# Pair 9's x scaled one step earlier, and pair 10's B and C loaded ahead of two stores, in a state-space scan followed by a bilinear feed-forward layer

## The chip, the cores and the metric

One core of one Trainium2 chip runs the whole program. The metric is the device time of one execution, in microseconds (us). Of the kernel before there are four such times: 125.66, 125.97, 127.06 and 128.04 us, with a median of 126.51 us.

## The reference, cut to what matters

The first half is a chunked state-space scan over x (4 batches, 8 heads, 768 tokens, 32 columns), decays a, and B and C (16 states a head). The second half multiplies two projections of its result and projects the product back.

```python
for c in range(nc):                       # chunks of 32 tokens
    cum = np.cumsum(la, axis=-1)          # la: log of the decays
    L = np.exp(cum[:, :, :, None] - cum[:, :, None, :]) * causal
    M = np.einsum('bhin,bhjn->bhij', Cc, Bc) * L
    y_intra = np.einsum('bhij,bhjd->bhid', M, xc)
    y_inter = np.einsum('bhin,bhnd->bhid', Cc, state) * np.exp(cum)[..., None]
    y[:, :, sl] = y_intra + y_inter
    state = decay_full * state + (Bc outer xc, decayed, summed over j)
...
a = x @ w_a          # 3072 tokens x 256 -> 1536
b = x @ w_b
return a * b @ w_out # -> 3072 x 256
```

## The kernel before, in words

**Tiling.** The kernel works with blocks of 128 tokens, so a sequence is six blocks. Two batches with all their heads make one *pair*; there are 12 pairs, 0 to 11, and pairs 2k and 2k+1 belong to block k. From pair 4 on, the path of one pair is this:

- `loads_bc(p)` (L699) allocates the pair's input tiles and issues four DMAs on SP's queue: C for two batches, then B for two batches, 64 KB each. `loads_x(p, nc.sync)` (L142) issues two DMAs of x, 128 KB each. The tiles `bn`, `cn` and `xn` have three buffers each.
- `prep(p)` (L853) works on POOL: C times its factors into `planes` (L279), B times its factors into `bm` (L287), two copies of `bm` into `planes` (L297). Then `turn(p)` (L331) issues one DMA transpose of `planes` on SP's queue, whose result is `turned`.
- `prep_x(p)` (L862) is one POOL instruction (L272): x times a constant, to f16. Its result is the weight operand of the pair's matmuls at L402.
- `stage(p, ...)` (L874) issues the pair's score matmuls on PE (L341), which read `turned`; `masked` multiplies them by the causal mask on DVE (L396) and puts feed-forward units of an earlier block between them (`bu`, `bunit`: matmuls at L650, copy on ACT at L598, product on DVE at L662).
- `group(blk)` (L866) issues, for both pairs of a block, the matmuls with the state (L491), those with x (L402, first all of the even pair and then all of the odd one), and the state's new sums (L430); ACT and DVE move the results to SBUF.
- `bout(blk, c)` (L668) is one output tile: twelve matmuls (L677), a copy on ACT into one of four `osb` buffers (L689), and a store of 128 KB on SP's queue (L690).

**What sets the order.** The schedule is written out by hand: each engine and each queue runs its instructions in the order of the program's text, and an instruction waits by semaphore for the data that it needs. SP's queue carries the loads, the transposes and the stores, one behind another. So a `turn` that waits for POOL holds back every load and store behind it, and a POOL instruction that waits for a load holds back all POOL work behind it.

**Around the change.** The text before runs `prep(9)`, the loads of x of pair 9, the rest of pair 7, `group(3)`, two output tiles `bout(2, 0)` and `bout(2, 1)`, and only then `loads_bc(10)`. After the scores of pair 8 it runs `prep_x(8)`, `prep(10)`, `loads_bc(11)` and `loads_x(10)`. `prep_x(9)` stands in the loop, behind the scores of pair 9 (L977, first round). `group(4)`, which needs x of pairs 8 and 9, follows later in that round.

Of the kernel before, what the change touches and what calls it, by code (L numbers as in the profile page):

```python
# [28 lines left out]
def kernel(  # L29
# [100 lines left out]
    def tiles(p):  # L130
        Bn = inp.tile([128, H, 2, N], f32, name="bn", tag="bn")
        Cn = inp.tile([128, H, 2, N], f32, name="cn", tag="cn")
        Xn = inp.tile([128, H, 2, D], f32, name="xn", tag="xn")
        pair_in[p] = (Bn, Cn, Xn)
# [4 lines left out]
    def load1(eng, p, which, bt, i0=0, n=64):  # L139
        blk, bp = divmod(p, NBP)  # L140
        if p >= P0:
            return eng.dma_start(  # L142
                by_token(pair_in[p][which])[:, bt],
                (B, C, x)[which][2 * bp + bt, :, blk * Q : (blk + 1) * Q, :].rearrange("h q n -> q h n"),
            )
        src = (B, C, x)[which][2 * bp + bt, :, blk * Q + 2 * i0 : blk * Q + 2 * i0 + 2 * n, :]
        return eng.dma_start(
            pair_in[p][which][64 * bt + i0 : 64 * bt + i0 + n].rearrange("i h r n -> i h (r n)"),
            src.rearrange("h (i r) n -> i h (r n)", r=2),
        )  # L150
# [114 lines left out]
    def scale_x(p, eng):  # L265
        X16 = mid.tile([128, H, 2, D], f16, name="x16", tag="x16")
        xo, xi = X16.rearrange("p h r d -> p (h r d)"), pair_in[p][2].rearrange("p h r d -> p (h r d)")
        st.setdefault(p, {})["X16"] = X16
        if eng is nc.scalar:
            nc.scalar.mul(xo, xi, XS)  # L270
        else:
            eng.tensor_scalar(xo, xi, XS, None, ALU.mult)  # L272

    def scale_bc(p, which, eng, factor=None):
        blk, bp = divmod(p, NBP)
        name, f = (("bm", fB), ("cm", fC))[which]
        raw = by_token(pair_in[p][which]) if p >= P0 else pair_in[p][which].rearrange("p h r n -> p r h n")
        if p >= P0 and which:
            eng.tensor_tensor(  # L279
                out=planes[p % 2][:, 4:6].rearrange("p t (h n) -> p t h n", n=N),  # L280
                in0=raw,
                in1=f[:, blk, :, bp].unsqueeze(3).broadcast_to((128, 2, H, N)),
                op=ALU.mult,
            )
            return
        m_ = mid.tile([128, 2, H, N], f16, name=name, tag=name)
        eng.tensor_tensor(  # L287
            out=m_,
            in0=raw,
            in1=(f[:, blk, :, bp] if factor is None else factor).unsqueeze(3).broadcast_to((128, 2, H, N)),  # L290
            op=ALU.mult,
        )
        st.setdefault(p, {})[name] = m_
        if p >= P0:
            dst = planes[p % 2][:, 0:4].rearrange("p (t e) (m f n) -> p t e m f n", e=2, f=2, n=N)
            for e in range(2):
                eng.tensor_copy(dst[:, :, e, :, e], m_.rearrange("p t (m f) n -> p t m f n", f=2)[:, :, :, e])  # L297
# [31 lines left out]
    def turn(p):  # L329
        T_ = mid.tile([128, 6, 128], f16, name="turned", tag="turned")  # L330
        nc.sync.dma_start(T_, planes[p % 2].rearrange("p a c -> p (a c)"), transpose=True)  # L331
        st[p]["BT"] = T_[:, 0:4].rearrange("p (t e) k -> p e t k", e=2)
        st[p]["CT"] = T_[:, 4:6]
# [32 lines left out]
    def product(p, m):  # L366

        if p >= P0:
            return (
                st[p]["T1"][:, 2 * m : 2 * m + 2].rearrange("p e t q -> p (e t) q"),  # L370
                SC[m].rearrange("p (c q) -> p c q", q=Q),
            )
        return (
            st[p]["T1"][:, 2 * m : 2 * m + 2].rearrange("p e r q -> p e (r q)"),
            SC[m].rearrange("p (e c) -> p e c", e=2),
        )
# [8 lines left out]
    def mask(out_in, by_pool=False, by_token=False):  # L385
        o_, i_ = out_in
        if by_token:
            c_ = causal_q.unsqueeze(1).broadcast_to((128, 4, Q))
        else:
            c_ = causal.rearrange("p r q -> p (r q)").unsqueeze(1).broadcast_to((128, 2, 2 * Q))  # L390
        if by_pool:
            tmp = mid.tile([128, *c_.shape[1:]], f32, name="tmp", tag="tmp")
            nc.scalar.copy(tmp, i_)  # L393
            nc.gpsimd.tensor_tensor(out=o_, in0=tmp, in1=c_, op=ALU.mult)  # L394
        else:
            nc.vector.tensor_tensor(out=o_, in0=i_, in1=c_, op=ALU.mult)  # L396
# [155 lines left out]
    def state_spread(p):  # L552
        blk, bp = divmod(p, NBP)
        if p + NBP < P0:
            Sbd = mid.tile([128, 2, H * D], f16, name="sbd", tag="sbd")
            nc.gpsimd.tensor_tensor(
                out=Sbd.rearrange("p t (m c) -> p t m c", m=4),
                in0=U32[:, p].unsqueeze(2).broadcast_to((128, 2, 4, 2 * D)),
                in1=maskbd.rearrange("p (m e) d -> p m (e d)", e=2).unsqueeze(1).broadcast_to((128, 2, 4, 2 * D)),
                op=ALU.mult,  # L560
            )
        else:
            Sbd = mid.tile([128, 2, 2 * D], f16, name="spair", tag="spair")
            nc.gpsimd.tensor_tensor(
                out=Sbd.rearrange("p t (e d) -> p t e d", e=2),
                in0=U32[:, p].rearrange("p t (e d) -> p t e d", e=2),
                in1=par.unsqueeze(1).unsqueeze(3).broadcast_to((128, 2, 2, D)),
                op=ALU.mult,
            )
        if blk + 1 < NG:  # L570
            nc.gpsimd.tensor_tensor(
                out=gU[:, p + NBP],
                in0=U32[:, p],
                in1=G[:, 2 * bp : 2 * bp + 2, blk + 1].unsqueeze(2).broadcast_to((128, 2, 2 * D)),
                op=ALU.mult,
            )
        st.setdefault(("S", p + NBP), {})["Sbd"] = Sbd
# [86 lines left out]
    def bgo(blk, *ks):  # L664
        for k in ks:
            bunit(blk, k)()
# [25 lines left out]
    def loads_bc(p):  # L692
        if p < NP:
            tiles(p)
            for w in (1, 0):
                for bt in range(2):
                    load1(nc.sync, p, w, bt)

    def loads_x(p, eng=None):  # L699
        if p < NP:  # L700
            for bt in range(2):
                load1(eng or nc.gpsimd, p, 2, bt)
# [150 lines left out]
    def prep(p, spread=()):  # L853
        if p < NP:
            scale_bc(p, 1, nc.gpsimd)
            scale_bc(p, 0, nc.gpsimd)
            turn(p)
        for q in spread:
            if q // NBP < NBLK - 1:
                state_spread(q)  # L860

    def prep_x(p):  # L862
        if p < NP:
            scale_x(p, nc.gpsimd)

    def group(blk):  # L866
        for p in range(blk * NBP, (blk + 1) * NBP):
            pull(p)
        outputs(blk)
        if blk < NBLK - 1:  # L870
            for p in range(blk * NBP, (blk + 1) * NBP):
                state_sums(p, (0,))
# [11 lines left out]
    def masked(p, ms, *units):  # L884
        for i in range(max(len(ms), len(units))):
            h = units[i]() if i < len(units) else None
            if i < len(ms):
                mask(product(p, ms[i]), by_token=True)
            if h:
                h()  # L890
# [4 lines left out]
    def bu(blk, *ks):  # L895
        return [lambda k=k: bunit(blk, k) for k in ks]
# [61 lines left out]
    prep(8)  # L958
    prep(9)
    loads_x(9, nc.sync)  # L960
    masked(7, (0, 1, 2), *bu(2, 5, 6, 7, 8, 9, 10, 11))
    group(3)
    bout(2, 0)
    bout(2, 1)
    loads_bc(10)

    stage(8, True, (6, 7))
    prep_x(8)
    prep(10)
    loads_bc(11)  # L970
    loads_x(10, nc.sync)
# [2 lines left out]
    for blk in range(4, NBLK):  # L974
        pB = blk * NBP + 1
        stage(pB, False)
        prep_x(pB)  # L977
        loads_x(pB + 2, nc.sync)
        prep(pB + 2)
        masked(pB, (0, 1))  # L980
        bout(blk - 2, 2)
        masked(pB, (2, 3), *bu(blk - 1, 6, 7, 8, 9))
        group(blk)
        bout(blk - 2, 3)
        bgo(blk - 1, 10, 11)
        if blk + 1 < NBLK:
            stage(pB + 1, False, (pB - 1, pB))
            prep_x(pB + 1)
            masked(pB + 1, (0, 1))
            bout(blk - 1, 0)  # L990
            masked(pB + 1, (2,))
            bout(blk - 1, 1)
            masked(pB + 1, (3,), *bu(blk, 0, 1, 2, 3, 4, 5))
# [40 lines left out]
```

## Time and profile before

| | |
|---|---|
| four runs | 125.66, 125.97, 127.06, 128.04 us, median 126.51 |
| the profiled execution's own time | 125.66 us |
| its span in the profile | 123.9 us |
| PE busy (matmuls) | 118.8 us, 96% of the span |
| PE weight loads | 81.3 us, 66% |
| DVE, ACT, POOL busy | 85.3, 71.9, 67.2 us |
| POOL's x scaling (L272) | 7 instructions, mean 1491 ns |
| granted PE clock | full in all 40 slices |
| x, B and C loads on SP's queue | median 3.6, 3.1 and 3.7 us from issue to landing |
| the transposes on SP's queue | 8, median 3.1 us from issue to landing |

The profile is one execution, and it is the fastest of the four times. Its span leaves out 1.76 us of the execution's time (125.66 less 123.9). Times inside the trace are counted from the span's start. Durations of instructions are those of the hardware; a POOL duration is rough, and the ends of matmuls are modelled, so that gaps on PE are read from the starts. A row of the timeline gives start, duration, engine, line and what is written and read; behind it, in brackets, the idle time before it and what ended it.

### The profile page before, as it was taken

Reading aid. Unit: us, or ns where it says so; the run is one execution under the profiler, and the core shown is the slowest. Engines: PE = TensorE matmul, PEld = TensorE weight load, DVE = VectorE, ACT = ScalarE, POOL = GpSimd, SP = SyncE. Lnnn points to the kernel's source line nnn. Section 1 sums busy time; section 2 is a strip of 40 time slices with the busy share of each in tenths; the row PEclk is TensorE's granted clock in tenths of the full one; section 3 lists DMA queues with packets and bytes.
Section 4 is the critical chain, followed back from the end, with each engine's and each line's share of the span. In section 5 each row is a group of like instructions: output and inputs, shape, how many; then the busy total and the mean of one; then the engine's idle time right before and its main releaser. Section 6 shows DMA issues by size and latency. Waiting matters only on the chain.

```text
span 123.9 us, 3757 instructions
## 1 busy us (share of the span) xinstructions
PE 118.8 (96%) x1455; PEld 81.3 (66%) x1455; DVE 85.3 (69%) x162; ACT 71.9 (58%) x142; POOL 67.2 (54%) x113
## 2 busy tenths in 40 slices
PE   5999999999999999999999999999999999999990
PEld 2446889988889788744457455657464785555880
DVE  1786885785987579398984989847889444847100
ACT  0366754684646685778658756674637736556220
POOL 7999999949999369279942855426800000000000
PEclk9999999999999999999999999999999999999999
DMA  3999999996989699599973862579811012010122
GB/s 67 164 173 232 174 206 160 199 175 61 113 120 195 73 91 211 112 163 132 182 102 68 173 62 27 91 69 146 215 40 42 5 42 85 0 48 0 42 92 78
DMA packets 63153, 13.73 MB, mean 111 GB/s; under 512 B 57904, under 2 KB 62672, under 8 KB 63136
## 3 DMA queue, kind: packets, MB, share of 16 engines
q1 hardware_dynamic: 58800, 9.01, 45.5%
q0 software_dynamic: 2336, 4.13, 18.3%
q10 hardware_dynamic: 2000, 0.36, 1.6%
q8 instruction: 11, 0.18, 0.7%
q14 instruction: 6, 0.05, 0.1%
HBM read 11.13 MB, written 3.15 MB: 115 GB/s over the span
## 4 chain that ended last, share of the span: by engine, by line
PE 76%; POOL 8%; DMA 6%; issue 2%; SPq 2%; ACT 1%; DVE 1%; POOLq 0%; ACTq 0%
PE ops L677 17%; PE aps L650 17%; PE bps L650 17%; PE aps L584 5%; PE bps L584 4%; DMA turned<-planes 4%; PE SC L210 3%; DMA cn<-in_C_dram 2%; PE ops L620 2%; PE SC L341 2%; POOL bm L287 2%; PE fps L238 2%; PE SC L402 1%; SPq L142 1%; POOL x L272 1%
## 5 line engine op out<-in xcount | busy, mean ns | idle before, releaser
L598 ACT COPY asb<-aps 128x512 f32<-128x512 f32 x72 | 42.0, 587 | 14.2 <-PE aps L650 9.7
L662 DVE TENSOR_TENSOR hkb<-bps,asb 128x512 f16<-128x512 f32 x48 | 32.3, 688 | 12.9 <-ACT asb L598 11.8
L650 PE MATMUL aps<-XB,Wa 128*128 128x512 f16 x96 | 28.6, 379 | 0.0
L650 PE MATMUL bps<-XB,Wb 128*128 128x512 f16 x96 | 28.5, 379 | 0.0
L677 PE MATMUL ops<-Wo,hkb 128*128 128x256 f16 (+1 forms) x204 | 22.5, 267 | 0.0
L677 PEld LDWEIGHTS <-hkb 128*128 128x128 f16 x204 | 18.5, 98 | 3.1
L396 DVE TENSOR_TENSOR t<-SC,causal_q 128x512 f16<-128x512 f32 x26 | 16.7, 682 | 5.1 <-PE SC L341 5.1
L605 DVE TENSOR_TENSOR hk<-bps,asb 128x512 f16<-128x512 f32 x24 | 16.2, 684 | 4.1 <-ACT asb L598 3.6
L650 PEld LDWEIGHTS <-Wb 128*128 128x128 f16 x96 | 9.9, 103 | 11.0 <-issue 0.3
L650 PEld LDWEIGHTS <-Wa 128*128 128x128 f16 x96 | 9.7, 103 | 9.1 <-issue 0.2
L584 PE MATMUL aps<-X2T,Wa 128*128 128x256 f16 x96 | 14.3, 273 | 0.3 <-DVE X2T L476 0.3
L689 ACT ACTIVATE osb<-ops 128x256 f32<-128x256 f32 (+1 forms) x16 | 6.0, 377 | 14.4 <-PE ops L677 14.2
L584 PE MATMUL bps<-X2T,Wb 128*128 128x256 f16 x96 | 14.1, 273 | 0.0
L620 PE MATMUL ops<-Wo,hk 128*128 128x256 f16 x96 | 11.6, 273 | 0.0
L272 POOL TENSOR_SCALAR x<-xn 128x512 f16<-128x512 f32 x7 | 10.4, 1491 | 1.4 <-DMA xn<-in_x_dram 1.0
L394 POOL TENSOR_TENSOR t<-tmp,causal_q 128x512 f16<-128x512 f32 x6 | 6.9, 1161 | 7.8 <-ACT tmp L393 7.7
L584 PEld LDWEIGHTS <-Wa 128*128 128x128 f16 x96 | 9.4, 104 | 1.5 <-DVE X2T L476 0.4
L584 PEld LDWEIGHTS <-Wb 128*128 128x128 f16 x96 | 9.8, 103 | 0.7
L620 PEld LDWEIGHTS <-hk 128*128 128x128 f16 x96 | 8.9, 98 | 1.5 <-DVE hk L605 0.2
L279 POOL TENSOR_TENSOR planes<-cn,fC 128x256 f16<-128x256 f32 x8 | 5.0, 624 | 7.2 <-DMA cn<-in_C_dram 7.1
L396 DVE TENSOR_TENSOR t<-SC,causal 128x512 f16<-128x512 f32 x13 | 8.2, 683 | 0.9 <-PE SC L356 0.8
L287 POOL TENSOR_TENSOR bm<-bn,fB 128x256 f16<-128x256 f32 x11 | 7.1, 648 | 2.9 <-DMA bn<-in_B_dram 1.5
(94 smaller groups left out, 124.5 us busy)
## 6 DMA issues: line engine op xcount, KB each, us to landing
out_dram<-osb SPq DMA_DIRECT2D x23, 128.0 KB, 1.9
xn<-in_x_dram SPq DMA_DIRECT2D x13, 128.0 KB, 3.6
bn<-in_B_dram SPq DMA_DIRECT2D x20, 64.0 KB, 3.1
xn<-in_x_dram POOLq DMA_DIRECT2D x10, 128.0 KB, 4.7
cn<-in_C_dram SPq DMA_DIRECT2D x18, 64.0 KB, 3.7
Wa<-in_moe_w_a_dram POOLq DMA_DIRECT2D x2, 384.0 KB, 5.6
Wb<-in_moe_w_b_dram POOLq DMA_DIRECT2D x2, 384.0 KB, 7.0
Wo<-in_moe_w_out_dram POOLq DMA_DIRECT2D x2, 384.0 KB, 6.9
```

What stands on the lines that cost most here:

```text
L272: eng.tensor_scalar(xo, xi, XS, None, ALU.mult)
L287: eng.tensor_tensor(out=m_, in0=raw, in1=(f[:, blk, :, bp] if factor is None else factor).unsqueeze(3).broadcast_to((128, 2, H, N)), op=AL ...
L394: nc.gpsimd.tensor_tensor(out=o_, in0=tmp, in1=c_, op=ALU.mult)
L396: nc.vector.tensor_tensor(out=o_, in0=i_, in1=c_, op=ALU.mult)
L584: nc.tensor.matmul(ps[:, kk * 2 * Q : (kk + 1) * 2 * Q], W[k // 6][:, f, k % 6 // 3 * 384 : (k % 6 // 3 + 1) * 384].rearrange("p (c kk) -> ...
L598: (nc.vector.tensor_copy if on_dve else nc.scalar.copy)(asb, a_ps)
L605: nc.vector.tensor_tensor(out=s["hk"][:, 2 * k2 : 2 * k2 + 2, :].rearrange("p k q -> p (k q)"), in0=b_ps, in1=asb, op=ALU.mult)
L620: nc.tensor.matmul(o_ps[:, 0:d_model], hk[:, k, bt * Q : (bt + 1) * Q], Wo[:, k, :], start=(k == 0), stop=(k == NK - 1), skip_group_check= ...
L650: nc.tensor.matmul(t_, W[k // 6][:, f, k % 6 // 3 * 384 : (k % 6 // 3 + 1) * 384].rearrange("p (c kk) -> p kk c", kk=3)[:, k % 3], XB[:, b ...
L662: return lambda: nc.vector.tensor_tensor(out=s["hk"][:, k], in0=ps[1], in1=asb, op=ALU.mult)
L677: nc.tensor.matmul(o_ps[:, 0:w], hk[:, k, c * Q : (c + 1) * Q], Wo[:, k, cs], start=(k == 0), stop=(k == NK - 1), skip_group_check=True,)
L689: nc.scalar.activation(out=o_sb[:, 0:w], in_=o_ps[:, 0:w], func=AF.Copy, scale=1.0 / (YS * YS))
```

## The change

Three places move; nothing is added and nothing is taken away. `loads_bc(10)` goes ahead of `masked(7, ...)`, `group(3)` and the two output tiles in the text: on SP's queue, its four loads now stand ahead of the two stores of `bout(2, 0)` and `bout(2, 1)`. `prep_x(9)` goes directly behind `prep_x(8)`: on POOL, ahead of pair 10's four instructions instead of behind them. The loop leaves out its own `prep_x` in its first round, since that was pair 9's.

```diff
     prep(8)
     prep(9)
     loads_x(9, nc.sync)
+    loads_bc(10)
     masked(7, (0, 1, 2), *bu(2, 5, 6, 7, 8, 9, 10, 11))
     group(3)
     bout(2, 0)
     bout(2, 1)
-    loads_bc(10)
 
     stage(8, True, (6, 7))
     prep_x(8)
+    prep_x(9)
     prep(10)
     loads_bc(11)
     loads_x(10, nc.sync)
@@
     for blk in range(4, NBLK):
         pB = blk * NBP + 1
         stage(pB, False)
-        prep_x(pB)
+        if blk > 4:
+            prep_x(pB)
         loads_x(pB + 2, nc.sync)
         prep(pB + 2)
```

In the compiled programs the order of instructions differs in two places only: on POOL, the scaling of pair 9's x stands ahead of `planes`, `bm` and two copies of pair 10; on SP, four loads stand ahead of two stores. PE, DVE and ACT run the same instructions in the same order.

## The prediction

> **What bounds the kernel now.** I read the page first: shares of the engines, granted clock and the chain that ended last.
>
> ```profile
> span 123.9 us, 3757 instructions
> ...
> PE 118.8 (96%) x1455; PEld 81.3 (66%) x1455; DVE 85.3 (69%) x162; ACT 71.9 (58%) x142; POOL 67.2 (54%) x113
> ...
> PEclk9999999999999999999999999999999999999999
> ...
> PE 76%; POOL 8%; DMA 6%; issue 2%; SPq 2%; ACT 1%; DVE 1%; POOLq 0%; ACTq 0%
> ```
>
> PE is nearly always busy, at full clock, and three quarters of the chain are its own. Then I read the chain in order of time. From 52.28 us on, up to the last copy on ACT, every piece of it is PE's. So a change in that stretch is worth what it takes out of the gaps between matmuls. Rows of the chain give start, length, engine and line:
>
> ```profile
> 64.12 0.56 PE SC L402 x32
> ...
> 78.66 0.63 PE SC L402 x32
> ...
> 82.55 0.33 PE SC L341 x16
> ...
> 90.79 0.33 PE SC L341 x16
> ...
> 96.24 0.56 PE SC L402 x32
> ```
>
> The 32 matmuls with x take 0.56 us in groups 3 and 5, but 0.63 in group 4. The instructions' starts show why: the 16 of pair 8 begin at 78.59, and the first of pair 9 at 78.89, 0.11 us after the one before it, where this step takes 0.05 in the other groups. PE waited there for x of pair 9. The POOL timeline tells where that came from:
>
> ```profile
> 71.34 1.49 POOL L272 TENSOR_SCALAR x<-xn 128x512 f16<-128x512 f32 x1
> 74.08 0.62 POOL L279 TENSOR_TENSOR planes<-cn,fC 128x256 f16<-128x256 f32 x1 [1.25 <-DMA cn<-in_C_dram]
> 76.04 0.62 POOL L287 TENSOR_TENSOR bm<-bn,fB 128x256 f16<-128x256 f32 x1 [1.34 <-DVE t L396]
> 76.73 0.53 POOL L297 COPY planes<-bm 128x128 f16<-128x128 f16 x2
> 77.34 1.49 POOL L272 TENSOR_SCALAR x<-xn 128x512 f16<-128x512 f32 x1
> 82.89 0.62 POOL L279 TENSOR_TENSOR planes<-cn,fC 128x256 f16<-128x256 f32 x1 [4.05 <-DMA cn<-in_C_dram]
> ```
>
> The row at 77.34 is pair 9's x; it ends at 78.83, when PE is already waiting. Before it POOL stood idle twice, 1.25 and 1.34 us, for pair 10's C and B. The second wait is put down to DVE, but the second B load landed at 75.89 (issued 73.04, 2.84 us), just before 76.04, and the DVE result that `bm` reads, a reciprocal, was there before 67. So it is the load. Last, SP's queue:
>
> ```profile
> 62.62 4.66 SPq L331 DMA_TRANSPOSE turned<-planes  x2
> 67.33 1.20 SPq L142 DMA_DIRECT2D xn<-in_x_dram  x2
> 68.63 1.18 SPq L690 DMA_DIRECT2D out_dram<-osb  x2
> 69.87 2.28 SPq L142 DMA_DIRECT2D cn<-in_C_dram  x2
> 72.19 1.43 SPq L142 DMA_DIRECT2D bn<-in_B_dram  x2
> 77.28 1.22 SPq L331 DMA_TRANSPOSE turned<-planes  x1
> 85.68 1.48 SPq L331 DMA_TRANSPOSE turned<-planes  x1
> ```
>
> Pair 10's loads (69.87, 72.19) stand behind two stores, then the queue idles from 73.62 to 77.28 until POOL has `planes` for the transpose. The chain to x of pair 9 is thus: stores, C and B loads, POOL's four instructions, x. It has no slack. x itself landed at 71.07 (second load issued 67.96, 3.11 us), 6.27 us before POOL took it up.
>
> **The change, part by part.** Nothing is added or removed, so only starts move.
>
> *Four loads past two stores, on SP.* The stores' issue takes 69.87 - 68.63 = 1.24 us, so the first C load goes out at 68.63. Bounds for the landing of the last B load: 1.24 us earlier (74.65) if the loads keep their pace; no earlier (75.89) if the DMA engines behind them set it. I take 1.24: the two stores no longer share the engines with the loads, which speaks for at least this. One issue in this stretch is long: the second C load's takes 1.78 us where most take 0.58. Should this long one fall on the last B load instead, its issue still ends 1.24 us sooner, so it is in the bound. No buffer holds the loads back: pair 10's tiles were last read by pair 7's POOL work, before 63 us.
>
> *Two stores past four loads.* They go out at about 72.4 instead of 68.63, into the idle stretch of SP, and end before 73.7. Nobody waits for them but the copy that takes the first one's `osb` buffer again, four tiles later, at 84.34 us. With the 4.28 us that the first took to land, that is 76.7, 7.6 us ahead. Cost nothing; if that cover were gone, ACT would wait.
>
> *x of pair 9 past four POOL instructions.* It starts when x of pair 8 ends, at 72.83 (71.34 + 1.49), in POOL's idle time, since its data is there at 71.07. It ends at 74.32 instead of 78.83. PE takes it at 78.8: 4.5 us of slack where there was none. Gain on PE: 0.63 - 0.56 = 0.07 us.
>
> The Trainium skill's page "SBUF — State Buffer", section "SBUF: two separate sides", speaks against a free move: VectorE and GpSimd share a pair of ports under an exclusive lock, and the later of the two is blocked for the other's whole instruction when VectorE runs in a two-port mode or reads two SBUF inputs. The seven x scalings, beside all kinds of DVE work, took 1486 to 1502 ns, so no row shows such a block; by the rule, as an estimate with one DVE product (688 ns) in the way, x would end at 75.0, still 3.8 us early.
>
> *What POOL and SP then do.* `planes` of pair 10 starts at 74.32 instead of 74.08, 0.24 later. From there, by the same steps in pair 9's rows of the trace: `bm` 0.58 later, the copies 0.69 after that, 0.53 long, the transpose 0.02 after. Sum from 74.32: 76.14, against 77.28. B is needed at 74.90, and 74.65 is in time. So pair 10's transpose goes out 1.14 us earlier, and all behind it on SP as well. If the loads gain nothing, `bm` stays at 76.04, the transpose at 77.28, and x of pair 9 has its slack all the same.
>
> *Does earlier help PE?* Pair 10's transpose landed at 80.08 and its scores start at 82.49: 2.4 us of slack, now 3.5. Pair 11's landed at 88.81 against 90.73: 1.9, now 3.0. x of pair 11 ends at 90.07 and is wanted at 96.2. All these are hidden by PE's own work already, so their gain is nothing.
>
> **Sum.** In the profiled execution: 125.66 - 0.07 = 125.59 us. The median of the four runs is 126.51, 0.85 above that execution. What the three other runs lost, no view shows. One candidate is this very chain: x of pair 9 had no slack, so every tenth of a microsecond by which the loads of pairs 9 and 10 fall behind PE goes straight into the time. B loads took 2.4 to 7.8 us to land in this profile, pair 10's last one 2.84, so there is room for delay. Bounds for what the change takes off the median: 0.07, if the extra time arises elsewhere (126.44), and 0.07 + 0.85 = 0.92, if all of it arises here (125.59). With no row to decide, I take the middle, 126.0.
>
> The Trainium skill's page "DMA: Bandwidth & Descriptors", section "Latency and other measured facts", gives an HBM access 0.2 us on average and 2 us at high load. An estimate by it: one late B load could cost the kernel before 1.8 us. No run here shows such a load at this place.
>
> **Rivals.**
>
> *More than the middle: the slower runs were slow here.* For it: the chain's zero slack, and a spread of 2.4 us over four runs while PE work is the same in all. Against it: the turned planes of pair 6 also arrive without slack (PE's weight loads wait 0.4 us for them, before 52.28), and the change does not touch these. If it holds and the kernel before is at the two slower runs when measured, 125.59 stands against 127.06 or 128.04: 1.47 or 2.45 us, 1.2 to 1.9%.
>
> *It does nothing: 0.07 us or less.* PE is bound, the other slacks were there, and the runs' spread is another's. 126.44 to 126.51. For it: the chain is PE's from 52.28 on.
>
> *Slower: x of pair 9 at the head of POOL's queue.* POOL must now wait for x's landing before pair 10's work, and for SP's transposes behind that. From the start X of x's scaling, the transpose follows at X + 1.49 + 0.58 + 0.69 + 0.53 + 0.02 = X + 3.31. It costs time once it pushes pair 11's transpose past its 1.9 us: X over 77.28 + 1.92 - 3.31 = 75.89, that is x landing 7.9 us after its issue at 67.96. Every us beyond is a us of PE. For 1% (1.27 us) X must be 77.16, a landing after 9.2 us. Against it: this landing took 3.11 us, the longest of any x load in the profile 7.1. Price where it decides: 127.8 us and above.
>
> **How the numbers follow.** The forecast, 125.59 to 126.44, gets 0.55; the first rival 0.20; nothing 0.10; the slower one, with any cost of the new order that the trace of before can't show, 0.15. About 1% is what a measurement of this kernel can tell from no change, since its four runs spread over 1.9%. Faster by over 1%: most of the first rival (0.18) and a little of the forecast (0.05), 0.23. Slower by over 1%: 0.15. Within: 0.62. The range goes beyond the bounds of the sum by a share of the runs' spread: 125.1 to 127.6.
>
> **What would show each step.** In the profile after: x of pair 9 on POOL at about 72.8, with no idle time before it; `planes` of pair 10 at 74.3 and its transpose at about 76.1; the C loads issued at about 68.6 and the stores at about 72.4; the group of 32 matmuls of group 4 at 0.56 us; and a span within 0.1 of 123.8 if PE ran as here. The forecast is wrong if PE's pieces in the chain are broken by a wait for a transpose or for x after 70 us, or if the median stays at 126.5 or more while the gap at group 4 is gone: then the spread of the runs has another source.

## The result, and the profile after

The changed kernel takes 125.88 us in the median of 53 executions (125.27 to 127.05); the kernel before takes 127.06 in the median of 79 (125.38 to 129.77). That is 1.18 us less, 0.93%. The comparison of the two leaves out executions more than 1.5% above the fastest of the same kernel, which are 32 of the 79 before (those above 127.26 us) and none of the 53 after; on what is left the ratio is 0.9968, with a 95% interval of 0.995 to 0.9986, which is 0.32% or 0.4 us. The lowest times differ by 0.11 us. So the change did little for an execution that went well, and took away the upper end: above 127.11 us lie 37 of the 79 executions before, and none of the changed kernel's 77 in this whole study (53 here, 12 and 12 below).

The profiled execution after took 126.40 us, so it is a later one than the profiled one of before (125.66). First the page's span, busy shares and chain:

```profile
span 124.7 us, 3757 instructions
...
PE 118.9 (95%) x1455; PEld 81.1 (65%) x1455; DVE 85.6 (69%) x162; ACT 72.0 (58%) x142; POOL 67.0 (54%) x113
...
PE 67%; DMA 13%; SPq 7%; POOL 6%; ACT 2%; issue 2%; DVE 1%; POOLq 0%; ACTq 0%
```

PE's work is the same to 0.1 us, and the chain has more DMA and SP in it. The place where this execution lost its time is on PE's timeline of the changed kernel, in group 2, ahead of everything that the change moved:

```profile
49.69 0.29 PE L402 MATMUL SC<-t,x 128*32 128x128 f16 x8 [0.61 <-POOL t L394]
```

The last eight matmuls of group 2 wait for pair 5's second mask on POOL. From start to start the step is 0.83 us instead of 0.05, so 0.78 us are lost. Pair 6's scores start at 53.04 here and at 52.28 in the profile of before, 0.76 later, and so does nearly all that follows. Then the rows of the chain that answer to those shown of before:

```profile
79.47 0.56 PE SC L402 x32
...
83.29 0.33 PE SC L341 x16
...
91.53 0.33 PE SC L341 x16
```

The 32 matmuls of group 4 take 0.56 us: the step of 0.07 is gone. POOL's timeline shows what stands behind it:

```profile
72.15 1.49 POOL L272 TENSOR_SCALAR x<-xn 128x512 f16<-128x512 f32 x1
74.56 1.49 POOL L272 TENSOR_SCALAR x<-xn 128x512 f16<-128x512 f32 x1 [0.93 <-DMA xn<-in_x_dram]
76.26 0.62 POOL L279 TENSOR_TENSOR planes<-cn,fC 128x256 f16<-128x256 f32 x1 [0.20 <-DMA cn<-in_C_dram]
77.56 0.62 POOL L287 TENSOR_TENSOR bm<-bn,fB 128x256 f16<-128x256 f32 x1 [0.68 <-DVE hkb L662]
78.24 0.53 POOL L297 COPY planes<-bm 128x128 f16<-128x128 f16 x2
```

x of pair 9 waits 0.93 us for its own load and still ends at 76.05, 3.6 us ahead of its matmuls at 79.63. The four instructions of pair 10 end at 78.77. In the old order x would have come behind them and would have ended past 80.2 even with the new order of loads. SP's queue:

```profile
69.90 1.20 SPq L142 DMA_DIRECT2D xn<-in_x_dram  x2
71.14 2.63 SPq L142 DMA_DIRECT2D cn<-in_C_dram  x2
73.81 1.32 SPq L142 DMA_DIRECT2D bn<-in_B_dram  x2
75.24 1.08 SPq L690 DMA_DIRECT2D out_dram<-osb  x2
78.79 1.22 SPq L331 DMA_TRANSPOSE turned<-planes  x1
...
87.99 1.23 SPq L331 DMA_TRANSPOSE turned<-planes  x1
```

The loads go out directly behind x's, and the stores into the queue's idle stretch, as the change says. But the queue as a whole is later than before: the loads of x go out at 69.90 instead of 67.33, 2.57 us, of which PE's own delay is 0.76. So relative to PE the queue lost 1.8 us in this execution. Pair 11's transpose lands at 90.75 (issue 87.99 and 2.76 us), 0.7 us before its scores: that is the slack left in this execution. (In the two further profiles of the changed kernel, `after_again` and `after_third` below, it is 0.4 and 3.3 us.)

### The profile page after: what moved, and what is told of

Same layout as the page of the kernel before. It is cut to its first block, busy times and chain, and to the rows that moved or that the text cites. A ratio compares the mean times of both kernels' runs of the same rounds, so it can differ in the third digit from the quotient of the medians.

```text
span 124.7 us, 3757 instructions
## 1 busy us (share of the span) xinstructions
PE 118.9 (95%) x1455; PEld 81.1 (65%) x1455; DVE 85.6 (69%) x162; ACT 72.0 (58%) x142; POOL 67.0 (54%) x113
## 4 chain that ended last, share of the span: by engine, by line
PE 67%; DMA 13%; SPq 7%; POOL 6%; ACT 2%; issue 2%; DVE 1%; POOLq 0%; ACTq 0%
PE ops L677 17%; PE aps L650 17%; PE bps L650 17%; DMA cn<-in_C_dram 7%; SPq L142 4%; DMA turned<-planes 3%; PE SC L210 3%; DMA bn<-in_B_dram 3%; PE aps L584 2%; PE bps L584 2%; PE SC L341 2%; SPq L147 2%; PE SC L402 1%; POOL x L272 1%; POOL t L394 1%
```

## The experiments

Theory A: x of pair 9 had no slack, so that whatever SP's loads lost against PE went through POOL into the time. Theory B: the earlier loads made the gain. Theory C: PE is the bound, and the difference is the spread of the executions. All medians below are over all executions of a kernel; a ratio is that of the comparison as above. The first four kernels ran on one chip, where the kernel before had a median of 128.08 us (29 executions, 126.54 to 129.83).

**Pair 9's x alone** (`x_only`):

```diff
     prep_x(8)
+    prep_x(9)
     prep(10)
...
-        prep_x(pB)
+        if blk > 4:
+            prep_x(pB)
```

> Only pair 9's x is moved on POOL; the four loads stay behind the two stores. Theory A (x of pair 9 had no slack, and what the loads lost went through it into PE): the 16 matmuls of pair 9 in group 4 never wait, and the median is that of the changed kernel, about 125.9 us, 0.4 to 0.9% below the kernel before. Theory B (the earlier loads make the gain): the median stays at that of the kernel before, 126.5 to 127.1. Theory C (PE bound, the difference is the spread of the runs): no difference either, and none in the other kernels of this set.

Measured: 127.25 us (12 executions), 0.83 less than the kernel before; the ratio is 0.9963 (0.9916 to 1.0009). PE doesn't wait for x in group 4. But its profile (127.28 us) has another wait, which theory A did not expect. The chain:

```profile
80.08 3.98 DMA turned<-planes
84.06 0.05 issue
84.11 0.40 PE SC L341 x16
```

PE starts the scores of pair 10 at 84.11, 0.63 us late (a step of 0.94 us where it is 0.31 without a wait), when pair 10's transpose has landed. Two things made it late. The loads, still behind the stores, held up POOL's work on `planes` and `bm`:

```profile
77.28 0.62 POOL L279 TENSOR_TENSOR planes<-cn,fC 128x256 f16<-128x256 f32 x1 [1.17 <-DMA cn<-in_C_dram]
78.84 0.62 POOL L287 TENSOR_TENSOR bm<-bn,fB 128x256 f16<-128x256 f32 x1 [0.94 <-DMA bn<-in_B_dram]
```

And the transpose itself took 3.98 us from issue to landing, where pair 10's took 2.77 to 2.80 us in the eleven other profiles. With 2.80 it would have landed at 82.88, 0.6 us ahead of the scores; why it was slow here, no view shows. In the three profiles of the changed kernel this transpose has 1.6 to 3.4 us of slack, more than the 1.2 us that it lost here.

**The four loads alone** (`loads_only`):

```diff
     loads_x(9, nc.sync)
+    loads_bc(10)
     masked(7, (0, 1, 2), *bu(2, 5, 6, 7, 8, 9, 10, 11))
     group(3)
     bout(2, 0)
     bout(2, 1)
-    loads_bc(10)
```

> Only the four loads are moved; pair 9's x stays behind pair 10's POOL work. Theory A: x of pair 9 still ends behind B of pair 10, but up to 1.2 us sooner than before, so only executions whose loads are later than that lose time: a part of the gain, median 126.0 to 126.7. Theory B: the whole gain, median about 125.9. Theory C: as the kernel before.

Measured: 127.87 us (12), 0.21 less than before; ratio 1.0015 (0.9967 to 1.0063). Its profile (128.17 us), the chain:

```profile
79.85 1.50 POOL x L272
81.35 0.04 issue
81.39 0.41 PE SC L402 x16
```

PE waited 0.98 us for x of pair 9, with the loads already moved. Theory B falls. In its profile each half alone leaves one wait: without the loads it is the transpose of pair 10, without x it is x.

**x of pair 9 scaled twice**, in the kernel before (`before_twice`) and in the changed one (`after_twice`). The second instruction writes a tile that nobody reads. The first added lines below stand in the kernel before, the last one in the changed kernel; the line that allocates the tile is left out.

```diff
+        if blk == 4:
+            nc.gpsimd.tensor_scalar(x_twice, pair_in[9][2].rearrange("p h r d -> p (h r d)"), XS, None, ALU.mult)
         prep_x(pB)
...
     prep_x(8)
+    nc.gpsimd.tensor_scalar(x_twice, pair_in[9][2].rearrange("p h r d -> p (h r d)"), XS, None, ALU.mult)
     prep_x(9)
```

> The kernel before, with pair 9's x scaled twice: a second instruction of 1.49 us, whose result nobody reads, directly ahead of the first on POOL. Theory A: no slack there, so PE starts pair 9's matmuls about 1.5 us later and the time rises by 1.3 to 1.5 us, over 1%. Theory C: PE has enough other work, a rise of less than 0.3 us.

> The changed kernel with the same second instruction of 1.49 us, directly ahead of pair 9's x. Theory A: x of pair 9 has 3 to 4.5 us of slack now, and the transposes of pairs 10 and 11 have 0.7 to 3.5: the median stays within 0.4 us of the changed kernel's 125.9, far below the kernel before with the doubled scaling. If the slack of pair 11's transpose is what comes next, some executions lose up to 0.8 us.

Measured: 131.70 us (8 executions) in the kernel before, 3.62 more than without, and 127.01 (12) in the changed one, 1.07 less than the plain kernel before (ratio 0.9938, 0.9891 to 0.9984). The ratio for the doubled kernel before is 1.0113 (1.0039 to 1.0187), 1.4 us, but it rests on two of the eight executions. So the same 1.49 us cost the old order about their own length in these two, and more in the other six. Theory C falls with this. What they cost the new order can't be sized, since the changed kernel itself was not run on that chip: 127.01 lies outside the 0.4 us about 125.9 that was expected, but on this chip the plain kernel before, too, lies 1.0 above its 127.06. In the profile (126.06 us) PE waits neither in group 4 nor at the scores of pairs 10 and 11. The lowest times of this chip point the same way: none of the 41 executions with x in its old place (the kernel before and `loads_only`) took less than 126.52 us, and three of the 24 with x moved (`x_only` and `after_twice`) took 125.50 to 126.06.

That the rise was more than 1.5 us was not expected. In the profile of the doubled kernel before (132.18 us), stretches with the busy times of PE, weight loads, DVE, ACT and POOL, and behind these the granted clock:

```profile
core 0: us, PE busy (x) PEld busy (x) DVE busy (x) ACT busy (x) POOL busy (x), PEclk, DMA share, GB/s
...
80.00:83.70 3.70, 0.38 (x24) 0.20 (x16) 0.69 (x1) 0.00 (x0) 3.51 (x4) 1.00 0.43 68
84.40:87.80 3.40, 3.40 (x15) 1.98 (x13) 0.95 (x4) 2.15 (x5) 0.62 (x1) 0.50 0.75 90
```

PE stood still for 3.51 us in group 4, until x of pair 9 was there, and then the granted clock was 0.50 for 3.41 us, which takes another 1.7 us of work. In six of the eight executions the mean clock was 0.974 to 0.987; the two at full clock took 128.25 and 129.18 us.

**The kernel before, with a profile of its own** (`before_again`), on a second chip, beside three others. There it ran 35 times for comparison, with a median of 127.02 (125.39 to 128.78).

> The kernel before once more, with a profile of its own. Theory A: PE waits in group 4, between the matmuls with x of pair 8 and those of pair 9, for 0.1 to 2 us, the longer the later this execution is above 125.66 us, and nowhere else after 70 us. Theory C (the executions' spread arises elsewhere): no more than the 0.05 us of the first profile there, at whatever time.

Measured: 126.22 us (12), against 127.02 of the same kernel. So a median of twelve executions is not better than 0.8 us, and the places of the waits tell more than the medians. The profiled execution took 127.10 us, and its chain shows the wait itself:

```profile
78.79 1.50 POOL x L272
80.29 0.04 issue
80.33 0.41 PE SC L402 x16
```

The step from pair 8's matmuls to pair 9's is 0.85 us here, 0.80 of it lost; in the first profile 0.06 were. After 70 us PE waits nowhere else. So 0.74 of the 1.44 us between the two executions (127.10 and 125.66) arose here. The other 0.70 arose earlier and outside the change: above all, PE lost 0.41 us in group 2, where the first profile lost none, and 0.42 ahead of pair 6's scores, where it lost 0.20.

**The changed kernel again** (`after_again`, and on a third chip `after_third`).

> The changed kernel, beside the kernel before on the same chip as the other three of this set. Theory A: 0.4 to 1.0% less than the kernel before in the median, with no wait of PE in group 4; below both halves of the change run alone. Theory C: as the kernel before.

> The changed kernel a second time on one chip with the next one, to tell the two apart. Theory A: 0.4 to 1.0% below the kernel before in the median, and no execution of it in the upper end of the kernel before's.

Measured: 126.27 us (12, up to 127.11) beside 127.02 before, ratio 0.9986 (0.9947 to 1.0025); and 126.13 (12, up to 126.74) beside 126.61 before (23 executions, up to 129.28), ratio 0.9995 (0.9954 to 1.0035). The medians are 0.75 and 0.48 lower, but both intervals include 1, and the twelve executions of `before_again` on the first of these chips (126.22) are as low as the changed kernel's: these sets alone show no gain in the median. The upper end is gone both times: 14 of the 35 executions before lie above 127.11 us on the one chip, and 10 of the 23 above 126.74 on the other. PE waits neither in group 4 nor at the scores of pairs 10 and 11 in either profile; they lose 0.63 and 0.29 us in group 2.

**Two steps further.** `late_stores` puts pair 3's two stores behind pair 9's B and C, in the manner of the change. `late_stores_dve` also gives pair 5's second mask to DVE.

```diff
     group(2)
-    out_half(3, 0)
-    out_half(3, 1)
+    late = []
+    for bt in range(2):
+        o_ps = bank("ops")
+        out_mm(3, bt, o_ps, range(NK))
+        late.append(out_store(3, bt, o_ps))
...
     loads_bc(9)
+    for f in late:
+        f()
     prep(8)
```

> The changed kernel, with two more stores (pair 3's) put behind four more loads (pair 9's B and C) on SP's queue. If the queue's lateness, up to pair 11's transpose, is what still costs time, everything on it from pair 9 on comes about 1.2 us sooner, its slack at the scores of pairs 10 and 11 grows from 0.7 to 1.9 us, and the median falls by 0.1 to 0.4 us below the changed kernel's. If the change has already taken the last wait of this kind away, there is no difference (within 0.2 us).

> The version with pair 3's stores behind pair 9's B and C, once more. If the 0.2 us between it and the changed kernel in the first set was more than chance, it is again 0.1 to 0.4 us below, with the smaller spread; if not, they are within 0.1 us of each other or the other way round.

> As the one before, and one of pair 5's two masks on POOL (1.16 us there, with its copy on ACT) goes to DVE (0.68 us). In five of the six profiles PE waited 0.4 to 0.9 us at about 50 us, in group 2, for this second mask. If that wait goes, 0.3 to 0.8 us less than the changed kernel, and below both. If DVE's products come too late in its place, no gain or a loss of up to 0.5 us.

```diff
-    mask(product(5, 2), by_pool=True, by_token=True)
...
-    masked(5, (0, 1), *pu(3, 2, 3, 4, 5))
+    masked(5, (0, 1, 2), *pu(3, 2, 3, 4, 5))
```

Measured: 126.04 us (12) beside 126.27 of the changed kernel, and in the second set 126.10 (12, up to 127.27) beside 126.13; the ratios to the kernel before are 0.9954 (0.9916 to 0.9993) and 1.0000 (0.9966 to 1.0034). On POOL, x of pair 9 follows x of pair 8 with no wait and `planes` starts at 74.94, where the changed kernel has 75.91 on the same chip, and pair 11's transpose lands 2.6 us ahead of its scores instead of 0.4: in this profile the queue's slack grew, and the time did not follow. This kind of wait has been used up: in all seven profiles of kernels with both halves of the change PE waits neither in group 4 nor at the scores of pairs 10 and 11. `late_stores_dve` took 126.36 us (12, up to 128.23); in its profile the wait for the mask is gone, and PE loses 0.19 us in group 2 (for POOL's `planes`) instead of the 0.65 of `late_stores`, but the median is no lower, and its profiled execution (127.46 us) was already 1.9 us late at 22 us. It is inconclusive, the more so since `late_stores_again`, with the mask still on POOL, had no wait in group 2 either. No version that beats the changed kernel was found.

## Why the prediction was right or wrong

**What bounds the kernel, and the chain to x of pair 9.** Right. POOL took x up late for pair 10's loads, there was no slack, and the profile of before at 127.10 us shows the same chain with 0.80 us of loss instead of 0.06.

**The step of 0.07 us.** Right in kind and size for the profiled execution of before: 0.63 became 0.56.

**The median: the middle between 0.07 and 0.92.** This is the step that failed, as a term of the sum that was mis-sized: 0.51 us was to come off the median, and 1.18 did. The bound of 0.92 took the distance between the profiled execution and a median of four, 0.85; the median of 79 is 127.06, 1.40 above that execution. And with no row to decide, half of the distance was given to this chain. The one later execution of the kernel before that has a profile supports a half: 0.74 of its 1.44 us arose here. Half of 1.40, with the 0.07, gives 0.77. What the other 0.4 us are stays open: a larger share of this chain in other executions, the kernel's further waits, chance, or differences between chips (three of them gave 126.61, 127.02 and 128.08 us for the kernel before, and on which the 79 and the 53 ran is not on record). By the ratio of the executions that the comparison keeps, the gain is 0.4 us. That the upper end disappears, all three sets in which the changed kernel ran show.

The outcome lies nearer to the first rival, which had 0.20 and 1.47 us for a kernel before at 127.06, than to the 0.51. That the time of the changed kernel, forecast at 126.0, came out at 125.88 is luck: the median of four lay 0.55 under that of 79, and this nearly made up for the 0.67 by which the step was too small.

**Earlier loads gain nothing, since other slacks hide them.** Not safe in later executions. The slacks at the scores of pairs 10 and 11 were to grow from 2.4 and 1.9 us to 3.5 and 3.0. In the three profiles of the changed kernel they are 1.6 and 0.7, 1.7 and 0.4, and 3.4 and 3.3. With x moved alone, the transpose of pair 10 came 0.63 us late in the one execution that has a profile, with a landing that was itself 1.2 us longer than elsewhere. So the loads' move gives slack that some executions need, once x no longer holds PE back and gives the transpose time; how often they need it is not shown.

**Starts.** x of pair 9 was to start at 72.8 and pair 10's transpose at 76.1; the profile has 74.56 and 78.79. The terms between them hold: from x's start to the transpose the sum says 3.31, and the profile has 4.23, with 0.20 and 0.68 us of waits in it. What moved is the queue ahead, by 2.57 us, which one profile could not tell. In `after_third`, where the queue was early, the working holds: x follows x of pair 8 with no wait, `planes` starts at 74.83 and the transpose at 76.64, with PE 0.36 us later than in the profile of before.

**The slower rival.** Its mechanism is real: POOL waited 0.93 us for x's landing, with pair 10's work behind it. It stayed below its price: x's scaling started at 74.56, and the rival needed a start past 75.89, or 76.65 with PE's own delay of 0.76. In the profile with 1.49 us more at the same place, pair 11's transpose was still 0.8 us early.

**It does nothing.** Refuted: the interval of the ratio, 0.995 to 0.9986, leaves out 1, and the doubled scaling cost the old order 1.1% by the ratio and 3.6 us in the median.

## What to carry to other kernels

A chain that ends just when the busy engine needs it costs next to nothing in an early execution's profile (0.06 us here) and far more in a later one (0.80): look for chains without slack, not only for gaps, and take a spread of the times as a sign that there may be one. When work is moved away from such a chain, ask what had been given time by the old wait; here the transpose came next, and the second half of the change covered it. To find slack, double the suspected instruction in both orders and see whether the busy engine waits for it: 3.51 us in the old order here, none in the new one. Run both plain kernels on the same chip beside these, so that the times can be compared as well.

## What the runs showed of the hardware that was not expected

A pause of PE of 3.51 us was followed by half the granted clock for 3.41 us (matmuls of 512 columns 427 ns apart instead of 216), so the wait cost about half as much again. Waits of up to 0.98 us in the other profiles were followed by no such drop. The Trainium skill's page "TensorE: Matmul & The Clock Gate", Part 1 on the clock gate, puts the window at 3.4 us and lets an idle window bring half rate; this run agrees, with its 3.41 us.

The place of SP's queue against PE moved by 1.2 us from one execution of the same program to another: in the two profiles of the kernel before, the loads of pair 9's x went out at 67.33 and 69.22, 1.89 us apart, while the matmuls of group 4 began 0.71 us apart, at full clock in both. The second of these loads took 3.11 us to land in the one and 3.75 in the other.

Single issues on SP were long as well: 1.78 us for a C load of pair 10 at 70.37 in the profile of before and 1.97 for one at 71.14 in that of after, where most take about 0.6. Both fell together with a packet of 16 KB on an instruction queue, which began at 70.04 and 71.04. That the packet holds the issue up is not shown.
